# Output transposes behind a run of matmuls, first loads in order of arrival, and a hand-set GpSimd order, in a fused attention and gated-MLP kernel

## The chip, the cores and the metric

The kernel runs on one core of a Trainium2 chip. The metric is the device time of one launch in microseconds (us). The record marks a run as slow when it lies over 1.5% above the fastest of its kernel. Medians and ranges below take in all runs. The profiled span is 2 to 6 us shorter than the timed runs, because it goes from the first instruction to the last.

## The reference, cut to what matters

Attention is within chunks of 64 tokens, then a gated MLP whose gate mixes tokens through a 576 x 576 spatial matrix. Shapes: batch 8, 8 heads, sequence 576, head dimension 64, d_model 512, d_ff 1024, all float32.

```python
scores = scale * (q_c @ k_c.T); attn = softmax(scores); x = attn @ v_c     # per 64-token chunk
h = maximum(x @ w_in, 0)
u, v = h[..., :512], h[..., 512:]
v_n = (v - mean(v)) / sqrt(var(v) + 1e-6)
v_s = einsum('ts,bsd->btd', w_spatial, v_n) + b_spatial[None, :, None]
out = (u * v_s) @ w_out
```

## The kernel before

Work goes by 36 tiles of 128 tokens. For a tile, GpSimd casts q, k and v to bf16. TensorE transposes q and k (TR) and computes scores (QK) and outputs (AV), one step later. Two steps later it transposes the attention output (XT). Then the MLP's matmuls go into a queue (`fifo`) and are emitted by `fill` between the attention parts. They are HV for the half that is normalised, U for the other half, SP for the spatial mix and FIN for the last product. Normalisations (vn) are done on GpSimd in groups of five or four tiles (LN). Ten groups of five "ws" transposes bring the spatial matrix into two layouts. (The texts call the MLP's matmuls MoE matmuls.) TensorE's order is set by the program. The other engines' orders come from a scheduler.

```python
ps_tr = pool("ps_tr", 1, space=PSUM)       # ONE buffer: TR, XT and the ws transposes share it
ps_big = pool("ps_big", 3, space=PSUM)     # HV, U, SP, FIN
# ...
def ws_transpose(p, i):
    ps = ps_tr.tile([128, 1024], BF16, name="tr")
    # five transposes of ws_nat into ps, then
    nc.vector.tensor_copy(dst[:n, :], ps[:n, 0:S])
# ...
load(0); load_w_in(); load(1); load(2); load_ws(); load(3); load_w_out()    # load() also emits the casts
with tc.manual_schedule(engines={mybir.EngineType.PE}):
    # ten ws_transpose pushed, ready at 16 us of a planned clock
    for s in range(NT + 3):
        # ... load(s + 3)
        TR(s)
        XT(s - 2); after_xt(s - 2)         # pushes HV, and U for every fourth tile
        fill(1.5)
        QK(s)
        AV(s - 1)
        fill(1.5)
```

The softmax here doesn't subtract the row's maximum and nothing guards it: scores larger than these inputs give would overflow.

Of the kernel before, what the change touches and what calls it, by code (L numbers as in the profile page):

```python
# [9 lines left out]
BF16 = mybir.dt.bfloat16  # L10
# [6 lines left out]
def kernel(  # L17
# [11 lines left out]
    nc = tc.nc  # L29

    B, H, S, D = q.shape
# [3 lines left out]
    F = d_ff // 2  # L35
    NTOK = B * S
    NT = NTOK // 128
# [9 lines left out]
    persist = pool("persist", 1)  # L47
# [18 lines left out]
    identb = consts.tile([128, 128], BF16, name="identb")  # L66
# [4 lines left out]
    NVB = 6  # L71
    vaug = [persist.tile([128, H, 65], BF16, name=f"vaug{i}") for i in range(NVB)]
# [6 lines left out]

    w_in_sb = persist.tile([128, 4, d_ff], BF16, name="w_in_sb")  # L80
    w_out_sb = persist.tile([128, 4, d_model], BF16, name="w_out_sb")
    ws_nat = [persist.tile([128, S], BF16, name=f"ws_nat{i}") for i in range(5)]

    ws_full = [[persist.tile([128, S], BF16, name=f"wsf{p}_{i}") for i in range(4)]
               for p in (0, 1)]
    ws_tail = [persist.tile([128, S], BF16, name=f"wst{p}") for p in (0, 1)]

    def load_w_in():
        for cb in range(4):
            nc.gpsimd.dma_start(out=w_in_sb[:, cb, :], in_=moe_w_in[cb * 128:(cb + 1) * 128, :])  # L90

    def load_ws():
        for i in range(5):
            n = 128 if i < 4 else 64
            nc.gpsimd.dma_start(out=ws_nat[i][:n, :], in_=moe_w_spatial[i * 128:i * 128 + n, :])
        for p in (0, 1):
            nc.gpsimd.dma_start(out=ws_tail[p][64:65, :], in_=moe_b_spatial[None, :])

    def load_w_out():
        for jb in range(4):  # L100
            nc.gpsimd.dma_start(out=w_out_sb[:, jb, :], in_=moe_w_out[jb * 128:(jb + 1) * 128, :])

    def ws_transpose(p, i):

        if i < 4:
            s0, n, dst = i * 128 + 64 * p, 128, ws_full[p][i]
        else:
            s0, n, dst = (512 if p == 0 else 0), 64, ws_tail[p]
        ps = ps_tr.tile([128, 1024], BF16, name="tr")
        for tb in range(5):  # L110
            m = 128 if tb < 4 else 64
            nc.tensor.transpose(ps[:n, tb * 128:tb * 128 + m],  # L112
                                ws_nat[tb][:m, s0:s0 + n], identb[:m, :m])
        nc.vector.tensor_copy(dst[:n, :], ps[:n, 0:S])


    st = {}
# [8 lines left out]
    def load(t):  # L126
        f32 = {}
        for name, src in (("q", q), ("k", k), ("v", v)):
            f = att_in.tile([128, H, D], FP32, name=f"{name}f")
            for r0, n, b, s in pieces(t):  # L130
                nc.sync.dma_start(out=f[r0:r0 + n], in_=src[b, :, s:s + n, :].rearrange("h s d -> s h d"))  # L131
            f32[name] = f
        qb = att_bf.tile([128, H, D], BF16, name="qb")
        kb = att_bf.tile([128, H, D], BF16, name="kb")
        nc.gpsimd.tensor_copy(qb, f32["q"])  # L135
        nc.gpsimd.tensor_copy(kb, f32["k"])  # L136
        nc.gpsimd.tensor_copy(vaug[t % NVB][:, :, 0:64], f32["v"])  # L137
        st[t] = {"q": qb, "k": kb}

    def TR(t):  # L140
# [40 lines left out]
    def XT(t):  # L181
        x = st[t].pop("x")
        ps = ps_tr.tile([128, 1024], BF16, name="tr")
        for m in range(4):
            nc.tensor.transpose(ps[:, m * 128:(m + 1) * 128],  # L185
                                x[:, 2 * m:2 * m + 2, :].rearrange("p h d -> p (h d)"), identb)
        g, r = divmod(t, 4)
        nc.scalar.copy(xT[g][:, :, r * 128:(r + 1) * 128],  # L188
                       ps[:, 0:512].rearrange("p (m s) -> p m s", m=4))
# [25 lines left out]
    def ln_group(t):  # L215

        k0, j = divmod(t, 9)
        return (2 * k0, j, 5) if j < 5 else (2 * k0 + 1, j - 5, 4)

    def LN(grp):  # L220
        k0 = 9 * (grp // 2)
        n = 5 if grp % 2 == 0 else 4
        ts = [k0 + j + (0 if n == 5 else 5) for j in range(n)]
        m = mv.pop(grp)
        lnv = stat_pool.tile([128, n], FP32, name=f"lnv{n}")
        rstd = stat_pool.tile([128, n], FP32, name=f"rstd{n}")
        nmu = stat_pool.tile([128, n], FP32, name=f"nmu{n}")
        nc.scalar.activation(lnv, m[:, :, 1], AF.Ln, bias=eps_sb)
        nc.scalar.activation(rstd, lnv, AF.Exp, scale=-0.5)
        nc.vector.scalar_tensor_tensor(out=nmu, in0=m[:, :, 0], scalar=-1.0, in1=rstd,  # L230
                                       op0=ALU.mult, op1=ALU.mult)
        for j, t in enumerate(ts):
            vr = relu.pop(t)
            if t - k0 == 4:
                te = tail_pool.tile([128, F], BF16, name="tail_e")
                to = tail_pool.tile([128, F], BF16, name="tail_o")
                nc.gpsimd.memset(te[64:65, :], 1.0)
                nc.gpsimd.memset(to[64:65, :], 1.0)
                nc.gpsimd.tensor_scalar(te[0:64], vr[0:64], rstd[0:64, j:j + 1], nmu[0:64, j:j + 1],
                                        op0=ALU.mult, op1=ALU.add)  # L240
                nc.vector.tensor_scalar(to[0:64], vr[64:128], rstd[64:128, j:j + 1], nmu[64:128, j:j + 1],
                                        op0=ALU.mult, op1=ALU.add)
                tail[grp], tail[grp + 1] = te, to
            else:
                y = vn_pool.tile([128, F], BF16, name="vn")
                nc.gpsimd.tensor_scalar(y, vr, rstd[:, j:j + 1], nmu[:, j:j + 1],  # L246
                                        op0=ALU.mult, op1=ALU.add)
                vn[t] = y
# [50 lines left out]
    def push(ready, cost, emit, after=None):  # L299
        fifo.append([ready, seq[0], cost, emit, after])  # L300
        seq[0] += 1
# [8 lines left out]
    def fill(quota):  # L310
        got = 0.0
        while got < quota:
            ok = [x for x in fifo if x[0] <= clock[0]]
            if not ok:
                break
            it = min(ok, key=lambda x: x[1])
            run(it)
            got += it[2]
# [3 lines left out]
    def after_hv(t):  # L322
        hv_done.add(t)
        grp = ln_group(t)[0]
        n = 5 if grp % 2 == 0 else 4
        k0 = 9 * (grp // 2) + (0 if n == 5 else 5)
        if all(x in hv_done for x in range(k0, k0 + n)):
            LN(grp)
            ln_done.add(grp)
            try_sp()  # L330

    sp_pushed = set()

    def try_sp():
        for b in range(B):
            if b in sp_pushed or b not in ln_done or (b % 2 and b - 1 not in ln_done):
                continue
            last_g = (b * S + S - 1) // 512
            if any((g, fb) not in u_done for g in range(last_g + 1) for fb in range(4)):
                continue  # L340
            sp_pushed.add(b)
            ready = clock[0] + 5.0
            for half in (0, 1):
                for db in range(4):
                    push(ready, 0.62, lambda b=b, half=half, db=db: SP(b, half, db),
                         lambda b=b, half=half, db=db: after_sp(b, half, db))
# [20 lines left out]
    def after_xt(t):  # L367
        push(clock[0] + 1.0, 0.87, lambda t=t: HV(t), lambda t=t: after_hv(t))
        if t % 4 == 3:
            g = t // 4  # L370
            for fb in range(4):
                push(clock[0] + 1.0, 0.87, lambda g=g, fb=fb: U(g, fb),
                     lambda g=g, fb=fb: after_u(g, fb))

    PRE = 4
    load(0)
    load_w_in()
    load(1)
    load(2)
    load_ws()  # L380
    load(3)
    load_w_out()
    with tc.manual_schedule(engines={mybir.EngineType.PE}):
        for p in (0, 1):
            for i in range(5):
                push(16.0, 0.4, lambda p=p, i=i: ws_transpose(p, i))
        for s in range(NT + 3):
            if s + PRE < NT and s > 0:
                load(s + PRE - 1)
            if s == NT - PRE:  # L390
                load(NT - 1)
            if s < NT:
                clock[0] = max(clock[0], 4.0 + 3.6 * s)
                TR(s)
                clock[0] += T_TR
            if 0 <= s - 2 < NT:
                XT(s - 2)
                clock[0] += T_XT
                after_xt(s - 2)
            fill(1.5)  # L400
            if s < NT:
                QK(s)
                clock[0] += T_QK
            if 0 <= s - 1 < NT:
                AV(s - 1)
                clock[0] += T_AV
            fill(1.5)
        while fifo:
            ok = [x for x in fifo if x[0] <= clock[0]]
            run(min(ok, key=lambda x: x[1]) if ok else min(fifo, key=lambda x: (x[0], x[1])))  # L410


# [1 line left out]
_INS = ['q', 'k', 'v', 'moe_w_in', 'moe_w_spatial', 'moe_b_spatial', 'moe_w_out']  # L414
# [26 lines left out]
```

## Time and profile before

| | before |
|---|---|
| time, median (range) | 264.78 us (262.84 to 265.74) |
| profiled span | 259.8 us |
| busy: PE / DVE / ACT / POOL | 200.8 / 119.6 / 107.8 / 103.6 us |
| mean granted clock (see below) | 0.954 |
| qkT copy of tile 6 / 15 / 35 | 48.7 / 97.5 / 216.2 us |

PE is TensorE, DVE VectorE, ACT ScalarE and POOL GpSimd. The granted clock is the share of its full clock that TensorE got. VectorE copies the transposed q and k of each tile once, so the start of that copy says when a tile passed. The page's slices show the stages: 40 equal parts of the span, busy share in tenths, then the granted clock in tenths and the DMA share.

```profile
PE   0425657784887887888888888878888888999993
PEclk9999955997697999999999999999999999999999
DMA  7999999997793812995388968992996030041225
```

The reader should see TensorE half idle in the first eight slices while DMA is full, a clock that falls to 0.5 to 0.7 several times before 85 us, and then a steady 8 in TensorE's row that becomes 9 only near the end.

### The profile page before, as it was taken

To read this page: it belongs to the slowest core of one execution; us is meant where nothing else is said; L and a number is where in the kernel's file an instruction comes from. 1 tells how busy PE (TensorE), PEld (TensorE's weight loads), DVE (VectorE), ACT (ScalarE), POOL (GpSimd) and SP (SyncE) were. 2 spreads that over 40 slices of the span, in tenths; PEclk is the share of its full clock that TensorE was granted. 3 is DMA by queue.
4 is the path that set the end of the run, shared out by engine and by line. 5 is a ranking of instruction groups with operands and counts; after the bars stand their busy time and mean duration, and the time that the engine had idled before them with its cause. 6 is when DMAs were issued, how large, how long until landed. Compare 5 with 4: busy or idle time off the path is not lost.

```text
span 259.8 us, 5942 instructions
## 1 busy us (share of the span) xinstructions
PE 200.8 (77%) x2375; PEld 122.9 (47%) x2402; DVE 119.6 (46%) x305; ACT 107.8 (42%) x197; POOL 103.6 (40%) x173
## 2 busy tenths in 40 slices
PE   0425657784887887888888888878888888999993
PEld 0213444444354654564456445644564456446461
DVE  0222524637434743574257525663374447426160
ACT  1102101563454145526553564256624651661713
POOL 3757553308708093097007631275266000410400
PEclk9999955997697999999999999999999999999999
DMA  7999999997793812995388968992996030041225
GB/s 158 220 231 227 183 213 209 215 201 149 160 219 75 165 42 75 253 207 116 113 201 203 218 160 208 209 158 76 259 232 127 19 145 3 0 159 46 77 85 202
DMA packets 119594, 40.36 MB, mean 155 GB/s; under 512 B 113360, under 2 KB 114448, under 8 KB 119568
## 3 DMA queue, kind: packets, MB, share of 16 engines
q1 hardware_dynamic: 117696, 37.76, 66.7%
q0 software_dynamic: 1872, 2.24, 5.0%
q8 instruction: 18, 0.29, 0.5%
q14 instruction: 8, 0.07, 0.1%
HBM read 32.79 MB, written 9.44 MB: 163 GB/s over the span
## 4 chain that ended last, share of the span: by engine, by line
PE 56%; DVE 19%; POOL 6%; DMA 5%; SPq 5%; ACT 4%; issue 3%; ACTq 0%; POOLq 0%
PE big L285 12%; PE big L253 10%; PE big L269 10%; PE big L203 9%; DVE qkT L148 7%; SPq L131 5%; PE tr L185 5%; DVE bst L209 4%; PE tr L145 3%; DMA kf<-in_k_dram 3%; DVE gat L276 3%; ACT v_relu L206 3%; PE tr L112 2%; PE o L172 2%; PE sc L158 2%
## 5 line engine op out<-in xcount | busy, mean ns | idle before, releaser
L246 POOL TENSOR_SCALAR vn<-v_relu,rstd,nmu 128x512 bf16<-128x512 f32 x32 | 25.3, 799 | 78.5 <-DVE nmu L230 72.5
L188 ACT COPY xT<-tr 128x512 bf16<-128x512 bf16 x36 | 21.1, 586 | 66.5 <-PE tr L185 66.5
L209 DVE BATCH_NORM_STATS2 bst<-v_relu 128x6 f32<-128x512 f32 x36 | 24.9, 692 | 42.5 <-ACT v_relu L206 42.5
L269 PE MATMUL big<-wsf,vn 128*128 128x288 bf16 x256 | 40.3, 286 | 0.1
L203 PE MATMUL big<-w_in_sb,xT 128*128 128x512 bf16 x130 | 38.8, 417 | 1.3 <-issue 0.8
L148 DVE COPY qkT<-tr 128x1024 bf16<-128x1024 bf16 x36 | 24.7, 685 | 32.5 <-PE tr L145 32.5
L185 PE MATMUL tr<-identb,x 128*128 128x128 bf16 x144 | 14.8, 229 | 31.4 <-DVE qkT L148 31.4
L276 DVE TENSOR_TENSOR gat<-big,uT 128x288 bf16<-128x288 f32 (+8 forms) x96 | 30.2, 351 | 15.4 <-PE big L269 14.3
L253 PE MATMUL big<-xT,w_in_sb 128*128 128x512 bf16 x137 | 34.4, 380 | 0.4
L285 PE MATMUL big<-w_out_sb,gat 128*128 128x512 bf16 (+1 forms) x154 | 34.1, 381 | 0.4
L135 POOL CAST qb<-qf 128x512 bf16<-128x512 f32 x36 | 22.1, 614 | 30.3 <-DMA qf<-in_q_dram 24.1
L162 ACT ACTIVATE eT<-sc 128x512 bf16<-128x512 f32 x36 | 21.4, 595 | 26.9 <-PE sc L158 26.9
L206 ACT ACTIVATE v_relu<-big 128x512 f32<-128x512 f32 x36 | 21.5, 597 | 26.4 <-PE big L203 23.8
L185 PEld LDWEIGHTS <-x 128*128 128x128 bf16 x144 | 11.6, 102 | 36.1 <-issue 34.1
L269 PEld LDWEIGHTS <-vn 128*128 128x128 bf16 x256 | 23.9, 97 | 7.8 <-DVE gat L276 0.4
L288 ACT COPY o_sb<-big 128x512 f32<-128x512 f32 x36 | 21.1, 586 | 15.6 <-PE big L285 15.2
L136 POOL CAST kb<-kf 128x512 bf16<-128x512 f32 x36 | 22.1, 614 | 13.4 <-DMA kf<-in_k_dram 13.2
L137 POOL CAST vaug<-vf 128x512 bf16<-128x512 f32 x36 | 22.2, 616 | 8.3 <-DMA vf<-in_v_dram 8.1
L178 DVE TENSOR_TENSOR x<-o,rz 128x512 bf16<-128x512 f32 x36 | 24.9, 691 | 0.9
L255 ACT ACTIVATE uT<-big 128x512 bf16<-128x512 f32 x36 | 21.4, 596 | 9.3 <-PE big L253 9.3
L145 PE MATMUL tr<-identb,qb 128*128 128x128 bf16 x144 | 15.2, 233 | 8.3 <-POOL qb L135 7.2
L203 PEld LDWEIGHTS <-xT 128*128 128x128 bf16 x144 | 14.0, 105 | 14.7 <-issue 3.9
(39 smaller groups left out, 193.5 us busy)
## 6 DMA issues: line engine op xcount, KB each, us to landing
out_dram<-o_sb SPq DMA_DIRECT2D x36, 256.0 KB, 2.1
qf<-in_q_dram SPq DMA_DIRECT2D x32, 256.0 KB, 4.8
kf<-in_k_dram SPq DMA_DIRECT2D x32, 256.0 KB, 5.1
vf<-in_v_dram SPq DMA_DIRECT2D x32, 256.0 KB, 5.2
w_in_sb<-in_moe_w_in_dram POOLq DMA_DIRECT2D x4, 256.0 KB, 5.4
qf<-in_q_dram SPq DMA_DIRECT2D x8, 128.0 KB, 4.7
kf<-in_k_dram SPq DMA_DIRECT2D x8, 128.0 KB, 4.8
vf<-in_v_dram SPq DMA_DIRECT2D x8, 128.0 KB, 4.5
```

Source lines behind the costliest of these rows:

```text
L145: nc.tensor.transpose(ps[:, c:c + 128], st[t][name][:, 2 * m:2 * m + 2, :].rearrange("p h d -> p (h d)"), identb)
L148: nc.vector.tensor_copy(qkT, ps)
L178: nc.vector.tensor_tensor(x, o[:, :, 0:64], rz.to_broadcast([128, H, D]), op=ALU.mult)
L185: nc.tensor.transpose(ps[:, m * 128:(m + 1) * 128], x[:, 2 * m:2 * m + 2, :].rearrange("p h d -> p (h d)"), identb)
L203: nc.tensor.matmul(hv, xT[g][:, cb, r * 128:(r + 1) * 128], w_in_sb[:, cb, F:], start=(cb == 0), stop=(cb == 3))
L206: nc.scalar.activation(vr, hv, AF.Relu)
L209: nc.vector.bn_stats(bst, vr)
L246: nc.gpsimd.tensor_scalar(y, vr, rstd[:, j:j + 1], nmu[:, j:j + 1], op0=ALU.mult, op1=ALU.add)
L253: nc.tensor.matmul(hu, w_in_sb[:, cb, fb * 128:(fb + 1) * 128], xT[g][:, cb, :], start=(cb == 0), stop=(cb == 3))
L269: nc.tensor.matmul(vs[:, 0:HS], lhsT, rhs, start=(i == 0), stop=(i == 4))
L276: nc.vector.tensor_tensor(gat[b][:, db, half * HS + done:half * HS + done + n], vs[:, done:done + n], uT[g][:, db, r:r + n], op=ALU.mult)
L285: nc.tensor.matmul(po[r0:r0 + n, :], gat[b][:, jb, s:s + n], w_out_sb[:, jb, :], start=(jb == 0), stop=(jb == 3))
```

## The change

There are three intents. XT goes behind the run of MLP matmuls, so VectorE's copy out of the single buffer lies beside them. The first tiles are loaded ahead of the weights, and the program's planned clock follows expected arrivals. GpSimd's order is set by hand, with a group's normalisations (`LN_apply`) emitted at the start of the next step, ahead of the cast of tile s+1.

```diff
+    def load_w_in(part, c0, c1): ...      # three transfers in place of four
+    def load_ws(): ...                    # one transfer and a tail in place of five
 ...
-            ready = clock[0] + 5.0
+            ready = clock[0] + 6.0
 ...
-    load(0); load_w_in(); load(1); load(2); load_ws(); load(3); load_w_out()   (cut)
-    with tc.manual_schedule(engines={mybir.EngineType.PE}):
+    ARR = [6.7, 11.0, 18.0, 21.5, 25.0, 32.0, 35.5]
+    with tc.manual_schedule(engines={mybir.EngineType.PE, mybir.EngineType.Pool}):
+        for t in range(PRE):
+            load(t)
+        cast(0, (after_cast0,))            # w_in's transfers between these casts
+        cast(1)
-                push(16.0, 0.4, lambda p=p, i=i: ws_transpose(p, i))
+                push(31.0, 0.4, lambda p=p, i=i: ws_transpose(p, i))
 ...
+            while ln_todo:
+                LN_apply(ln_todo.pop(0))
+            if 0 < s and s + 1 < NT:
+                cast(s + 1)                # load_ws after tile 3, load_w_out after tile 5
             TR(s)
-            XT(s - 2)
             fill(1.5)
+            XT(s - 2)
             QK(s)
             AV(s - 1)
+            # an extra fill and an early XT where the next tile is not expected for 2 us
             fill(1.5)
```

More of the change, by code (lines that the diff above doesn't have):

```diff
@@ L81 @@
     w_out_sb = persist.tile([128, 4, d_model], BF16, name="w_out_sb")
-    ws_nat = [persist.tile([128, S], BF16, name=f"ws_nat{i}") for i in range(5)]
+    ws_nat = persist.tile([128, 5, S], BF16, name="ws_nat")
     ws_full = [[persist.tile([128, S], BF16, name=f"wsf{p}_{i}") for i in range(4)]
@@ L86, with load_w_in @@
     ws_tail = [persist.tile([128, S], BF16, name=f"wst{p}") for p in (0, 1)]
-    def load_w_in():
-        for cb in range(4):
-            nc.gpsimd.dma_start(out=w_in_sb[:, cb, :], in_=moe_w_in[cb * 128:(cb + 1) * 128, :])
+    w_in_v = moe_w_in.rearrange("(c p) f -> p c f", p=128)
+    def load_w_in(part, c0, c1):
+        cols = slice(F, 2 * F) if part == "v" else slice(0, F)
+        nc.gpsimd.dma_start(out=w_in_sb[:, c0:c1, cols], in_=w_in_v[:, c0:c1, cols])
     def load_ws():
-        for i in range(5):
-            n = 128 if i < 4 else 64
-            nc.gpsimd.dma_start(out=ws_nat[i][:n, :], in_=moe_w_spatial[i * 128:i * 128 + n, :])
+        nc.gpsimd.dma_start(out=ws_nat[:, 0:4, :],
+                            in_=moe_w_spatial[0:512, :].rearrange("(i p) s -> p i s", p=128))
+        nc.gpsimd.dma_start(out=ws_nat[:64, 4, :], in_=moe_w_spatial[512:S, :])
         for p in (0, 1):
@@ L99, in load_w_out @@
     def load_w_out():
-        for jb in range(4):
-            nc.gpsimd.dma_start(out=w_out_sb[:, jb, :], in_=moe_w_out[jb * 128:(jb + 1) * 128, :])
+        nc.gpsimd.dma_start(out=w_out_sb, in_=moe_w_out.rearrange("(c p) f -> p c f", p=128))
     def ws_transpose(p, i):
@@ L112, in ws_transpose @@
             nc.tensor.transpose(ps[:n, tb * 128:tb * 128 + m],
-                                ws_nat[tb][:m, s0:s0 + n], identb[:m, :m])
+                                ws_nat[:m, tb, s0:s0 + n], identb[:m, :m])
         nc.vector.tensor_copy(dst[:n, :], ps[:n, 0:S])
@@ L132, in load, with cast @@
             f32[name] = f
+        st[t] = {"f32": f32}
+    def cast(t, after_each=()):
+        f32 = st[t].pop("f32")
         qb = att_bf.tile([128, H, D], BF16, name="qb")
         kb = att_bf.tile([128, H, D], BF16, name="kb")
-        nc.gpsimd.tensor_copy(qb, f32["q"])
-        nc.gpsimd.tensor_copy(kb, f32["k"])
-        nc.gpsimd.tensor_copy(vaug[t % NVB][:, :, 0:64], f32["v"])
+        for dst, name in ((qb, "q"), (kb, "k"), (vaug[t % NVB][:, :, 0:64], "v")):
+            nc.gpsimd.tensor_copy(dst, f32[name])
+            for f in after_each:
+                f(name)
         st[t] = {"q": qb, "k": kb}
@@ L218, in ln_group @@
         return (2 * k0, j, 5) if j < 5 else (2 * k0 + 1, j - 5, 4)
+    ln_st = {}
     def LN(grp):
@@ L231, in LN, with LN_apply @@
                                        op0=ALU.mult, op1=ALU.mult)
+        ln_st[grp] = (k0, ts, rstd, nmu)
+    def LN_apply(grp):
+        k0, ts, rstd, nmu = ln_st.pop(grp)
         for j, t in enumerate(ts):
@@ L328, in after_hv @@
             LN(grp)
+            ln_todo.append(grp)
             ln_done.add(grp)
@@ L332 @@
     sp_pushed = set()
+    ln_todo = []
     def try_sp():
@@ L375, with arrival, after_cast0 @@
     PRE = 4
-    load(0)
-    load_w_in()
-    load(1)
-    load(2)
-    load_ws()
-    load(3)
-    load_w_out()
-    with tc.manual_schedule(engines={mybir.EngineType.PE}):
+    ARR = [6.7, 11.0, 18.0, 21.5, 25.0, 32.0, 35.5]
+    def arrival(t):
+        return ARR[t] if t < len(ARR) else ARR[-1] + 3.5 * (t - len(ARR) + 1)
+    def after_cast0(name):
+        if name == "q":
+            load_w_in("v", 0, 2)
+        elif name == "k":
+            load_w_in("v", 2, 4)
+        else:
+            load_w_in("u", 0, 4)
+    with tc.manual_schedule(engines={mybir.EngineType.PE, mybir.EngineType.Pool}):
[3 more added lines that the diff above has]
+        cast(1)
         for p in (0, 1):
             for i in range(5):
-                push(16.0, 0.4, lambda p=p, i=i: ws_transpose(p, i))
+                push(31.0, 0.4, lambda p=p, i=i: ws_transpose(p, i))
+        xt_next = 0
         for s in range(NT + 3):
-            if s + PRE < NT and s > 0:
+            if PRE <= s + PRE - 1 < NT and s > 0:
                 load(s + PRE - 1)
-            if s == NT - PRE:
-                load(NT - 1)
+            while ln_todo:
+                LN_apply(ln_todo.pop(0))
+            if 0 < s and s + 1 < NT:
+                cast(s + 1)
+                if s + 1 == 3:
+                    load_ws()
+                if s + 1 == 5:
+                    load_w_out()
             if s < NT:
-                clock[0] = max(clock[0], 4.0 + 3.6 * s)
+                a = arrival(s)
+                if a > clock[0]:
+                    fill(a - clock[0] - 0.3)
+                clock[0] = max(clock[0], a)
                 TR(s)
                 clock[0] += T_TR
-            if 0 <= s - 2 < NT:
-                XT(s - 2)
+            fill(1.5)
+            while xt_next <= s - 2 and xt_next < NT:
+                XT(xt_next)
                 clock[0] += T_XT
-                after_xt(s - 2)
-            fill(1.5)
+                after_xt(xt_next)
+                xt_next += 1
             if s < NT:
@@ L406 @@
                 clock[0] += T_AV
+                if s + 1 < NT and arrival(s + 1) > clock[0] + 2.0:
+                    fill(1.5)
+                    clock[0] += 0.5
+                    XT(s - 1)
+                    clock[0] += T_XT
+                    after_xt(s - 1)
+                    xt_next = s
             fill(1.5)
@@ L410 @@
             run(min(ok, key=lambda x: x[1]) if ok else min(fifo, key=lambda x: (x[0], x[1])))
+            while ln_todo:
+                LN_apply(ln_todo.pop(0))
 _INS = ['q', 'k', 'v', 'moe_w_in', 'moe_w_spatial', 'moe_b_spatial', 'moe_w_out']
```

## The prediction

> **What bounds the kernel now.** I read the page's busy shares and slices first, then the windows by stage, then the waits of TensorE, then one step of the timeline. The windows (columns: span of the stretch, busy us of PE, PEld, DVE, ACT, POOL with counts, granted clock, DMA share, GB/s):
>
> ```profile
> 0.00:50.00 50.00, 24.53 (x314) 16.66 (x317) 16.32 (x40) 8.98 (x15) 27.44 (x53) 0.86 1.10 206
> 50.00:100.00 50.00, 39.65 (x517) 24.13 (x521) 24.87 (x60) 23.19 (x44) 23.78 (x39) 0.90 0.73 140
> 100.00:150.00 50.00, 42.80 (x562) 26.47 (x568) 26.92 (x69) 24.62 (x46) 21.93 (x35) 1.00 0.84 183
> 150.00:225.00 75.00, 63.31 (x808) 39.09 (x815) 39.69 (x102) 36.07 (x67) 23.99 (x39) 1.00 0.60 136
> 225.00:260.00 35.00, 30.50 (x182) 16.57 (x183) 11.82 (x35) 14.98 (x27) 6.51 (x9) 1.00 0.28 105
> ```
>
> There are three stages. To 50 us the DMA engines are full (share 1.10) and TensorE is half idle: 50 - 24.5 = 25.5 us. From 50 to 225 us no engine but TensorE is near full; it idles 175 - 145.8 = 29.2 us. After 225 us it is dense, and its 4.5 us of idle is the last copy and store. Busy time here is the union of overlapping records, so I use it for gaps, not for peak. What fills the gaps, from the table of waits over the whole span (us in total, times, longest):
>
> ```profile
> POOL vn L246 <- DVE nmu L230: 72.5, 7, 23.5
> PE tr L185 <- DVE qkT L148: 31.4, 34, 2.4
> PE tr L145 <- POOL qb L135: 7.2, 3, 4.7
> PE tr L145 <- POOL kb L136: 6.8, 3, 3.9
> ```
>
> Restricted to 50 to 225 us, the second row is 27.4 us over 29 waits, so 27.4 of the 29.2 us idle in the long middle stage is one single wait. The timeline shows what it is:
>
> ```profile
> 120.80 0.39 PE L145 MATMUL tr<-identb,kb 128*128 128x128 bf16 x4
> 121.22 0.69 DVE L148 COPY qkT<-tr 128x1024 bf16<-128x1024 bf16 x1 [0.56 <-PE tr L145]
> 121.97 0.38 PE L185 MATMUL tr<-identb,x 128*128 128x128 bf16 x4 [0.78 <-DVE qkT L148]
> 122.19 1.89 PE L253 MATMUL big<-xT,w_in_sb 128*128 128x512 bf16 x7
> ```
>
> The pool of transposes holds one PSUM buffer. TensorE transposes q and k of tile s into it (TR), and the next thing in its program is the transpose of output tile s-2 (XT) into the same buffer. So it stands still for VectorE's copy (0.69 us plus hand-over), with eight MoE matmuls ready behind it. A step, from one qkT copy to the next, is 5.67 us where nothing else disturbs it (121.22 back from 115.55).
>
> **What the Trainium skill says.** "PSUM — Partial Sum Buffer", section "Engine vs sequencer instructions": matmuls start and complete in program order, and the queues of ScalarE, VectorE and GpSimd are strict FIFO. The trace agrees: XT holds back the ready L253 matmuls. "Perfetto Trace Analysis", section "Matmuls" under "Optimizing Tensor Performance": independent groups should rotate through PSUM banks so that evacuation of one overlaps matmuls of the next. The one "tr" buffer doesn't, at 0.78 us a time. "TensorE: Matmul & The Clock Gate", Part 1: the clock is halved until the array has been busy for about 3.4 us. The first group of four q transposes takes 0.60 us, against 0.39 us in the step above, so the DMA-fed beginning does run cold. "DMA: Bandwidth & Descriptors", section "Why small descriptors are slow (HBM only)": there is a fixed cost per packet and per descriptor at 256 B. The page counts 113360 of 119594 packets under 512 B, and the saturated rate is 206 GB/s.
>
> **Part 1, XT behind the fill.** The order becomes TR(s), a run of about 1.7 us of MoE matmuls, XT(s-2), QK(s), AV(s-1), another run. The copy (0.78 us of wait, up to 1.3 us where VectorE is late) then lies beside 1.7 us of matmuls. Nothing is added. QK reads qkT, long done, and XT's buffer is copied out by ScalarE (0.59 us) under QK, AV and the next run, 0.75 + 1.7 us, before the next TR. The undisturbed step becomes 5.67 - 0.78 = 4.89 us. I count 90% of the 27.4 us as recovered, **-24.5 us**: some steps have an empty queue of MoE work early (the short steps near 48, 62 and 78 us), and in steps of spatial matmuls VectorE runs at about 90%. There six evictions of about 0.48 us plus qkT 0.69, x 0.69 and reciprocal 0.20 make 4.5 us in 4.89.
>
> **Part 2, the beginning.** Weights now follow the casts: w_in in three transfers after the three casts of tile 0, the spatial weights after tile 3's casts, w_out after tile 5's. About 1.33 + 1.05 MB of reads, at 206 GB/s some 11.6 us of DMA, move behind the first tiles. Before, qkT copies of tiles 4 and 5 stand at 35.1 and 46.2 us. A tile is 786 KB, 3.8 us at 206 GB/s, and the change expects tiles 4 and 5 at 25 and 32 us. The ten spatial-weight transposes (1.3 us each through the single buffer, 26 to 42 us before) remain, and they remain slow. By 50 us the kernel before has copied tile 6; I expect tile 8 or 9 after. Two to three tiles of work at about 3 us (attention 1.25, first matmul's two halves 0.87 + 0.87, by the chain's durations) are done earlier: **-8 us** of idle, including an extra XT placed where the next tile has not come.
>
> **Part 3, GpSimd by hand.** Before, casts may run ahead of a group's normalisations. In the new program order the normalisations of a group (LN_apply) stand ahead of the cast of the next tile but one. GpSimd cannot pass them. The chain of waits shows how late their input is:
>
> ```profile
> 186.89 0.88 PE big L203 x4
> 187.85 0.61 ACT v_relu L206
> 188.48 0.69 DVE bst L209
> 189.62 0.30 ACT lnv L228
> 190.53 0.16 DVE nmu L230
> ```
>
> From the end of the last group member's matmuls (187.77) to nmu's end (190.69) is 2.9 us. Then GpSimd works 4 x 0.80 = 3.2 us, or with tail and memsets 3.2 + 0.76 + 2 x 0.52 = 5.0 us, then two casts of 0.61 us. So the casts are done h + 7.5 or h + 9.3 us into a pair of steps, where h is when those matmuls ended, and TR wants them at 2 x 4.89 = 9.8 us. With h between 1.3 and 4.9 the stall is 0 to 2.6 us for groups of four tiles and 0.8 to 4.4 us for groups of five. Averaging about 1.1 and 2.7 over six groups that still have tiles behind them gives 11 us. Where h falls early it vanishes, and the wait for a clogged GpSimd (first row of the second table) that starved loads between 78 and 102 us goes, so I charge **+6 us** net.
>
> **Part 4, DMA in the middle.** In a 4.89 us step it must bring 786 KB (3.8 us) and store 256 KB (an estimate of 0.7 us, from 105 GB/s at share 0.28 in the last row of windows). That is 4.5 us, 92%. I charge **+3 us** for late tiles and VectorE-limited steps together.
>
> **Sum.** 259.8 - 24.5 - 8 + 6 + 3 = 236.3 us of span. The timed runs (262.84 to 265.74) stand 3 to 6 us above the profiled span, and the profiled run itself 2.1; I add 3. **Predicted: 239 us.**
>
> **Rivals.** (a) The wait only moves: GpSimd becomes the bound at each group. For it: the order is now forced and the working gives up to 4.4 us a group. Against: GpSimd is only 40% busy and has three cast buffers. If all 11 to 20 us fell on the path, 246 to 253 us. (b) DMA becomes the bound. For it: 92% in the middle and a full first stage. Inputs alone need 28.3 MB / 206 GB/s = 137 us, the weights about 13 (cast transfers' share), some 22 stores 15, so the last tile cannot come before about 166 us, and TensorE wants it near 172. Against: buffers reach up to seven tiles ahead. This would give 242 to 248 us. (c) All parts work and the early work makes the clock warm sooner (0.86 and 0.90 in the first two rows), while stalls vanish: 227 us. (d) XT's delay puts off HV and the MoE queue runs dry, so the gap is only moved: it would stay near 255 us. The queue is rarely dry after 80 us (all 5.67 us steps hold full runs), so this is unlikely.
>
> **Range and chances.** (c) and (a) set the edges: 227 to 251 us. The removed wait alone is 10% of the span, so faster by over 2% (under 259.8 us) gets 0.95, same 0.04, slower 0.01.
>
> **What would show it.** Right: the row "tr L185 <- qkT" falls from 31.4 us to under 5; undisturbed steps are near 4.9 us; TensorE idle in the first 50 us falls to 15-20 us; new rows of "tr L145 <- qb" or "kb" of 1 to 4 us appear after each group's normalisations. Wrong: steps stay over 5.4 us, or waits for qb and kb in the middle add up to more than 12 us, or they trace back to transfers in flight rather than to L246.

## The result, and the profile after

The changed kernel takes 249.01 us in the median (248.57 to 251.08) against 264.78 us. The ratio is 0.9429, 95% interval 0.9353 to 0.9504. Here and below a ratio is the mean time of one kernel's fast runs over that of the other's in the same rounds, so it is not quite the ratio of the medians quoted. The time is inside the predicted range (227 to 251 us), but near its slow end. The sum foretold 23.5 us off the span, and 12.5 us came (259.8 to 247.3).

The windows of the changed kernel (columns as in the prediction):

```profile
0.00:50.00 50.00, 24.93 (x310) 16.35 (x310) 15.58 (x39) 8.59 (x14) 22.13 (x41) 0.89 1.09 194
50.00:100.00 50.00, 40.80 (x551) 25.25 (x551) 25.47 (x62) 21.65 (x42) 25.11 (x42) 0.84 0.86 169
100.00:150.00 50.00, 48.05 (x604) 29.32 (x603) 28.75 (x73) 27.37 (x52) 22.41 (x36) 1.00 0.77 175
150.00:225.00 75.00, 72.40 (x822) 42.76 (x821) 42.51 (x109) 42.03 (x80) 28.62 (x45) 1.00 0.62 149
225.00:260.00 35.00, 18.15 (x122) 11.09 (x120) 7.84 (x24) 5.91 (x11) 2.44 (x4) 0.96 0.18 68
```

TensorE's busy time rose by 5.3 us in the 50 us from 100 and by 9.1 us in the 75 us from 150, but only by 0.4 and 1.2 us in the two windows before. (The 0.89 in the first row counts the time before the clock's first record, at 31.8 us, as 1.00.) Progress by tiles says it more sharply. The qkT copy of tile 15 starts at 97.51 us before and at 97.50 us after. **By then nothing had been gained.** From tile 15 to tile 35 the kernel before takes 118.7 us, 5.94 a tile. The changed one takes 104.5 us, 5.23 a tile. That is 14.2 us, more than the whole gain: what comes after the start of tile 35's copy takes 45.3 us, against 43.6 before.

The waits of the changed kernel (us in total, times, longest), to set against the four in the prediction:

```profile
POOL vn L258 <- DVE nmu L238: 64.3, 6, 16.2
PE tr L151 <- POOL qb L141: 17.2, 9, 5.1
PE tr L151 <- POOL kb L141: 5.8, 9, 2.9
PE tr L191 <- DVE qkT L154: 2.3, 3, 1.0
```

XT's wait fell from 31.4 to 2.3 us, but the waits for casts of q and k rose from 14.0 to 23.0 us. In both kernels 14.0 us of these fall in the first 50 us; the new 9.0 us come later. One step of the timeline shows the first (instructions of TensorE and VectorE alone; a bracket gives the engine's idle time and who ended it):

```profile
122.24 0.39 PE L151 MATMUL tr<-identb,kb 128*128 128x128 bf16 x4
122.46 1.03 PE L265 MATMUL big<-xT,w_in_sb 128*128 128x512 bf16 x4
122.66 0.69 DVE L154 COPY qkT<-tr 128x1024 bf16<-128x1024 bf16 x1 [1.34 <-PE tr L151]
123.42 1.05 PE L297 MATMUL big<-w_out_sb,gat 128*64 128x512 bf16 x8
124.40 0.40 PE L191 MATMUL tr<-identb,x 128*128 128x128 bf16 x4
```

While VectorE copies, TensorE does MLP matmuls, and XT no longer carries an idle time in brackets. An undisturbed step (tile 15 to 16) is 4.73 us, against 5.67 before.

The second, at tile 9, from the timeline (lines left out between). It shows one of the places where the first half's gain went:

```profile
62.65 3.22 POOL L258 TENSOR_SCALAR vn<-v_relu,rstd,nmu 128x512 bf16<-128x512 f32 x4 [12.35 <-DVE nmu L238]
62.86 0.42 PE L178 MATMUL o<-vaug,eT 64*64 64x65 bf16 x16
67.71 0.60 POOL L141 CAST qb<-qf 128x512 bf16<-128x512 f32 x1
68.37 0.61 PE L151 MATMUL tr<-identb,qb 128*128 128x128 bf16 x4 [5.09 <-POOL qb L141]
69.33 1.91 PE L209 MATMUL big<-w_in_sb,xT 128*128 128x512 bf16 x4
73.02 1.03 PE L209 MATMUL big<-w_in_sb,xT 128*128 128x512 bf16 x4
```

GpSimd was idle for 12.35 us, waiting for the group's nmu, with the cast of tile 9 behind that wait in its order. Then it spent 5.1 us on the group. TensorE had an empty queue of MLP work and stood still for 5.09 us. The clock fell in this stall, at 65.9 us, and was 0.50 from 66 to 72 us: four HV matmuls took 1.91 us, and 1.03 once the clock was back. At tile 13 the same thing cost 2.19 us.

### The profile page after: what moved, and what is told of

Its sections match the earlier page's. It is cut to its first block, busy times and chain, and to the rows that moved or that the text cites. A ratio compares the mean times of both kernels' runs of the same rounds, so it can differ in the third digit from the quotient of the medians.

```text
span 247.3 us, 5971 instructions
## 1 busy us (share of the span) xinstructions
PE 204.3 (83%) x2402; PEld 124.8 (50%) x2402; DVE 120.2 (49%) x305; ACT 105.6 (43%) x197; POOL 100.7 (41%) x166
## 3 DMA queue, kind: packets, MB, share of 16 engines
q1 hardware_dynamic: 117696, 37.76, 69.7%
## 4 chain that ended last, share of the span: by engine, by line
PE 49%; POOL 7%; issue 5%; DMA 4%; DVE 3%; SPq 2%; ACT 1%; POOLq 0%; ACTq 0%
PE big L281 13%; PE big L297 10%; PE big L265 9%; PE big L209 8%; DMA vf<-in_v_dram 4%; PE tr L151 4%; PE o L178 2%; PE tr L191 2%; PE sc L164 2%; SPq L132 2%; POOL vn L258 2%; POOL kb L141 2%; POOL qb L141 2%; DVE bst L215 1%; POOL vaug L141 1%
## 5 line engine op out<-in xcount | busy, mean ns | idle before, releaser
L258 POOL TENSOR_SCALAR vn<-v_relu,rstd,nmu 128x512 bf16<-128x512 f32 x32 | 25.1, 796 | 81.4 <-DVE nmu L238 64.3
L209 PE MATMUL big<-w_in_sb,xT 128*128 128x512 bf16 x144 | 40.6, 414 | 0.0
L265 PE MATMUL big<-xT,w_in_sb 128*128 128x512 bf16 x144 | 35.6, 390 | 0.0
L297 PE MATMUL big<-w_out_sb,gat 128*128 128x512 bf16 (+1 forms) x160 | 34.5, 381 | 0.0
L168 ACT ACTIVATE eT<-sc 128x512 bf16<-128x512 f32 x36 | 22.0, 611 | 17.5 <-PE sc L164 17.5
L281 PEld LDWEIGHTS <-vn 128*128 128x128 bf16 x256 | 23.7, 97 | 10.6 <-DVE gat L288 2.5
L151 PEld LDWEIGHTS <-qb 128*128 128x128 bf16 x144 | 11.1, 105 | 25.2 <-POOL qb L141 19.2
L265 PEld LDWEIGHTS <-w_in_sb 128*128 128x128 bf16 x144 | 13.5, 100 | 14.7 <-issue 1.6
```

The costliest lines, as they stand in the source:

```text
L151: nc.tensor.transpose(ps[:, c:c + 128], st[t][name][:, 2 * m:2 * m + 2, :].rearrange("p h d -> p (h d)"), identb)
L168: nc.scalar.activation(eT, sc[:, :, 0:256], AF.Exp, scale=att_scale)
L209: nc.tensor.matmul(hv, xT[g][:, cb, r * 128:(r + 1) * 128], w_in_sb[:, cb, F:], start=(cb == 0), stop=(cb == 3))
L258: nc.gpsimd.tensor_scalar(y, vr, rstd[:, j:j + 1], nmu[:, j:j + 1], op0=ALU.mult, op1=ALU.add)
L265: nc.tensor.matmul(hu, w_in_sb[:, cb, fb * 128:(fb + 1) * 128], xT[g][:, cb, :], start=(cb == 0), stop=(cb == 3))
L281: nc.tensor.matmul(vs[:, 0:HS], lhsT, rhs, start=(i == 0), stop=(i == 4))
```

## The experiments

Twelve kernels ran, each on one chip. All gave correct results. Lines are compared within a call where possible, and across calls by their ratios to the kernel before. Timings are medians of four runs. The diffs are shortened.

### Which part carries the gain

**e1_xt_only**, the kernel before with one edit:

```diff
-            if 0 <= s - 2 < NT:
-                XT(s - 2); clock[0] += T_XT; after_xt(s - 2)
             fill(1.5)
+            if 0 <= s - 2 < NT:
+                XT(s - 2); clock[0] += T_XT; after_xt(s - 2)
             if s < NT:
                 QK(s)
```

> The kernel before with one edit: XT(s-2) stands behind the first run of MoE matmuls. Theory A (the move of XT carries the whole gain; the load order and the GpSimd order add nothing): the row of waits 'tr <- qkT' of XT falls from 31.4 us to under 4, and the time is 245 to 251 us, like the changed kernel's 249. Theory B (each of the three parts carries some): 254 to 259 us.

Measured: 243.31 us (242.62 to 244.52), ratio 0.9263 (0.9177 to 0.9348). This is below theory A's range: the one edit is faster than the whole change. Its waits of TensorE:

```profile
PE tr L145 <- POOL qb L135: 13.7, 7, 4.8
PE tr L145 <- POOL kb L136: 9.1, 6, 3.2
PE tr L185 <- DVE qkT L148: 2.3, 4, 0.8
```

XT's wait is gone here too (31.4 to 2.3). But 22.8 us now go to q and k casts, against 14.0 before. A faster TensorE reaches the casts sooner and waits there (15.7 us before 50 us, 7.1 us after). So 29.1 us of wait removed, less 8.8 us of new waiting, is 20.3 us, and the span fell by 18.1 (259.8 to 241.7).

**e2_xt_first**, the changed kernel with XT put back:

```diff
-            fill(1.5)
             while xt_next <= s - 2 and xt_next < NT:
                 XT(xt_next); ...
+            fill(1.5)
```

> The changed kernel with XT put back ahead of the run. Theory A: the XT wait is back at 27 to 32 us and the time is 262 to 268 us, no better than the kernel before. Theory B: 254 to 259 us, since the other two parts still give their share.

Measured: 283.64 us (282.52 to 283.88), ratio 1.0789 (1.071 to 1.0868). Both theories missed the time; the XT wait, 27.5 us, is in theory A's range. **Without the XT move the other two parts make the kernel 8% slower than it was.** Its waits:

```profile
PE tr L191 <- DVE qkT L154: 27.5, 32, 1.4
PE tr L151 <- POOL qb L141: 24.6, 8, 5.1
PE tr L151 <- POOL kb L141: 4.2, 5, 2.6
```

The casts cost 28.8 us here, 14.8 more than before, and the clock in the window from 50 to 100 us is 0.74 against 0.90. TensorE's busy time is 209.1 us against 200.8 for the same matmuls. The parts don't add. By the ratios the XT move is worth 1 - 0.9263 = 0.074 of some 262 us, or 19 us, in the old order, and 1.0789 - 0.9429 = 0.136, or 36 us, in the new one.

### GpSimd's order

**e3_pool_free** leaves GpSimd to the scheduler again:

```diff
-    with tc.manual_schedule(engines={mybir.EngineType.PE, mybir.EngineType.Pool}):
+    with tc.manual_schedule(engines={mybir.EngineType.PE}):
```

> The changed kernel with GpSimd's order left to the scheduler; the orders of all other engines are the same but for a few VectorE rows. Theory A (the hand order costs: TR of tile 9 waited 5.1 us and of tile 13 2.2 us for casts that stood behind a group's normalisations): those two waits shrink and the time is 242 to 247 us. Theory B (the hand order helps by letting normalisations come in time): 251 to 256 us, with new waits for qb or kb, or for vn.

Measured: 246.24 us (245.51 to 247.3), ratio 0.9377 (0.9304 to 0.945). It is inside theory A's range, but its interval overlaps the changed kernel's, so taken alone it decides nothing. Of theory A's two waits one is gone; that of tile 13 stayed at 2.19 us. The beginning was slower (tile 6 is copied at 52.3 us, against 47.4), so the time mixes a loss and a gain.

**e4_cast_first** changes two blocks' order in the hand order:

```diff
-            while ln_todo:
-                LN_apply(ln_todo.pop(0))
             if 0 < s and s + 1 < NT:
                 cast(s + 1)
                 ...
+            while ln_todo:
+                LN_apply(ln_todo.pop(0))
```

> The changed kernel with the cast of tile s+1 ahead of the waiting normalisations in GpSimd's hand order; only GpSimd's order changes. Theory A: the waits for qb at tiles 9 and 13 (5.1 and 2.2 us) and the idle DMA between 60 and 68 us go, with the cold clock that follows them: 241 to 246 us. Theory B: the normalisations come one cast (1.9 us) later and the MoE queue runs dry instead: 248 to 251 us.

Measured: 240.78 us (239.68 to 241.76), ratio 0.9165 (0.9092 to 0.9238). Theory A's range was met. TensorE's, ScalarE's and the DMA queue's orders are the same as in the changed kernel. The change's order, normalisations ahead of the cast, therefore cost 0.9429 / 0.9165, that is 2.9%. The waits for qb from 50 to 100 us, in the changed kernel and then in e4:

```profile
PE tr L151 <- POOL qb L141: 7.3, 2, 5.1
PE tr L151 <- POOL qb L141: 2.1, 1, 2.1
```

A hand order is not bad in itself: with the cast first it beats the scheduler's (e3) by 5.5 us on the same chip.

### The new beginning

**e5_old_start** gives the changed kernel the old beginning, the weights' old pieces among it, and keeps the hand order:

```diff
-        for t in range(PRE): load(t)
-        cast(0, (after_cast0,)); cast(1)
+        load(0); cast(0); load_w_in(); load(1); cast(1); load(2); load_ws(); load(3); cast(2); load_w_out()
-                push(31.0, 0.4, ...ws_transpose...)
+                push(16.0, 0.4, ...ws_transpose...)
-                a = arrival(s); fill(...); clock[0] = max(clock[0], a)
+                clock[0] = max(clock[0], 4.0 + 3.6 * s)
-                (the extra fill and early XT)
```

> The changed kernel with the beginning of the kernel before: weight transfers in their old pieces and places, spatial-weight transposes from 16 us on, the old pacing rule, no extra XT; GpSimd's hand order with normalisations ahead of casts stays. Theory A (the new beginning gives next to nothing, the forced order costs): 246 to 251 us, within 2% of the changed kernel's 249, with waits for qb and kb after 50 us of 5 us or more. Theory B (the new beginning saved the forecast 8 us and the forced order ate it): 254 to 259 us.

Measured: 247.93 us (247.47 to 248.23), ratio 0.9433 (0.9375 to 0.9491), against the changed kernel's 0.9429. Theory A: no difference, and 8.2 us of waits for qb and kb from 50 to 225 us.

**e6_old_start_cast_first** is e5 with the cast-first edit of e4.

> As e5_old_start, and the cast ahead of the normalisations as in e4_cast_first. It differs from e4_cast_first (240.8 us) by the beginning alone. Theory A: 240 to 244 us, as the XT move alone in the old order (243.3) with the free order replaced by a harmless one. Theory B (new beginning worth 8 us): 247 to 250 us.

Measured: 237.83 us (237.13 to 238.81), ratio 0.9041 (0.8973 to 0.911). It is below theory A's range, and 10.1 us faster than e5 on the same chip. So the order of normalisations and casts costs 4% under the old beginning too. Against e4 (0.9165), which differs by the beginning alone, the old beginning is, if anything, the better one. The intervals just overlap.

### The ten transposes of the spatial matrix

The forecast of 8 us for the beginning had failed, and the timeline of the changed kernel showed a chain there:

```profile
36.29 0.52 PE L113 MATMUL tr<-identb,ws_nat 128*128 128x128 bf16 x5 [1.12 <-DVE qkT L154]
36.84 0.46 DVE L115 COPY wsf<-tr 128x576 bf16<-128x576 bf16 x1 [0.61 <-PE tr L113]
37.35 0.52 PE L113 MATMUL tr<-identb,ws_nat 128*128 128x128 bf16 x5 [0.55 <-DVE wsf L115]
37.91 0.46 DVE L115 COPY wsf<-tr 128x576 bf16<-128x576 bf16 x1 [0.61 <-PE tr L113]
```

It goes on so to 50.2 us, broken only by one tile's transposes and scores: half a microsecond of TensorE, half a microsecond of waiting for the copy. The granted clock over 36 to 51 us was 0.59. Tile 6's casts were done at 38.3 us, and its TR started at 46.4.

**e7_ws_big** is e4 with one word changed for the ten:

```diff
     def ws_transpose(p, i):
-        ps = ps_tr.tile([128, 1024], BF16, name="tr")
+        ps = ps_big.tile([128, 1024], BF16, name="big")
```

> e4_cast_first with the ten spatial-weight transposes in the pool of three PSUM buffers instead of the single one shared with TR and XT. Theory A (the forecast saving at the beginning was lost to this serial chain, ten times 1.3 us from 36 to 50 us, in which tile 6's TR stood 8 us behind its casts): the ten take under 8 us, the qkT copy of tile 6 comes at 42 to 44 us instead of 47, and the time falls by 2 to 5 us to 236 to 239 us. Theory B (the beginning is bound by arrivals, so nothing is gained): 240 to 242 us.

Measured: 232.05 us (230.17 to 234.12), ratio 0.8807 (0.8721 to 0.8893). Theory A's direction, and more than its size: 3.9% against e4's 0.9165. In its timeline:

```profile
34.55 2.05 PE L113 MATMUL big<-identb,ws_nat 128*128 128x128 bf16 x20
35.58 1.54 DVE L115 COPY wsf<-big 128x576 bf16<-128x576 bf16 x4
```

Twenty transposes now take 2.05 us. All ten groups are through at 40.4 us, tile 6's copy comes at 39.6 us (47.0 in e4), tile 8's at 50.3 (61.2 in e4). From 31.3 us, where both have a record, to 50 us the clock is 1.00 (0.68 in e4). Shorter waits and a warm clock come together, and no run separates them.

**e8_ws_spread** also spreads the ten over about 35 us of the planned clock:

```diff
-                push(31.0, 0.4, lambda p=p, i=i: ws_transpose(p, i))
+                push(31.0 + 3.5 * (5 * p + i), 0.4, lambda p=p, i=i: ws_transpose(p, i))
```

> e7_ws_big with the ten spatial-weight transposes spread, one about every 3.5 us of the planned clock, instead of in a row. They are first needed near 75 to 90 us. Theory A: TR of tiles 6 and 7 no longer stands behind them, their copies come at 38 to 45 us, and the time is 234 to 238 us. Theory B (arrivals bind): as e4_cast_first, 240 to 242 us, TensorE simply waiting for casts instead.

Measured: 234.43 us (232.67 to 237.06), ratio 0.8855 (0.8773 to 0.8936). It is in theory A's range against e4, but it gains nothing over e7. With the three buffers, then, that the ten stand in a row costs nothing that these runs can tell. Spreading them in the single buffer was not run.

**e12_before_ws_big** makes e7's edit alone in the kernel before.

> The kernel before with the spatial-weight transposes alone moved to the pool of three buffers; XT stays ahead of the run. Theory A: the chain costs the same with or without the XT move, 251 to 257 us against 262 to 265. Theory B: 260 to 265 us, its waits lie beside the wait for arrivals.

Measured: 258.08 us (255.95 to 263.09), ratio 0.9799 (0.9713 to 0.9884). It lies between the two theories: 5.8 us by the medians, where theory A asked for 7 or more. The interval leaves a gain of 1.2 to 2.9%, and the verdict at 2% is unclear. Tile 6 is copied at 42.7 us against 48.7, but at tile 15 the lead is 4.2 us (93.3 against 97.5).

### Putting together

**e9_cast_two** is e7 with the casts one step further ahead (`cast(s + 2)` in step s, `cast(2)` in the prologue, the weight loads still after tiles 3 and 5):

```diff
-            if 0 < s and s + 1 < NT:
-                cast(s + 1)
+            if 0 < s and s + 2 < NT:
+                cast(s + 2)
```

> e7_ws_big (232.1 us) with the casts of a tile one more step ahead in GpSimd's order (cast s+2 in step s, ahead of the waiting normalisations). Theory A (in e7 tile 10's TR still waits 3.8 us for a cast that stands behind the first group's normalisations, so a cast further ahead takes that wait away): no wait for qb or kb over 1.5 us after 50 us, 227 to 230 us. Theory B (that wait was for the transfer, or the normalisations now come too late): 231 to 234 us.

Measured: 229.87 us (227.69 to 231.71), ratio 0.8724 (0.8644 to 0.8804). It has the lowest ratio of all, 7.5% under the changed kernel (0.8724 / 0.9429), but its interval overlaps those of e7, e8 and e10, so the step from e7 is not settled by the time. One wait over the bound set by theory A stayed: 2.30 us at tile 11, in place of 3.81 us at tile 10. The casts of the tile behind the normalisations still wait for the group's 4.9 us on GpSimd (56.2 to 61.1 us). Going a step further ahead moved the wait by a tile and made it shorter. The clock row is flat, where the kernel before dips several times. It is flat by record from 30.5 us on; before, four q transposes take 0.61 us, against 0.40 later. This profile is of the fastest of the four runs (227.69 us, mean clock 0.998; the others have 0.961 to 0.983):

```profile
PEclk9999999999999999999999999999999999999999
```

**e10_old_start_ws_big** is e7 with the old beginning (e6 with the ws edit).

> e7_ws_big with the beginning of the kernel before (weight transfers, pacing, no extra XT). Theory A (the new beginning is worth nothing in itself; e6 was no slower than e4): 229 to 233 us, within 2% of e7's 232. Theory B (the new beginning pays once the serial chain of spatial-weight transposes is out of the way, as forecast): 237 to 241 us.

Measured: 230.93 us (229.54 to 235.5), ratio 0.8775 (0.8689 to 0.886), against e7's 0.8807. Theory A. The new load order does bring tile 4 forward (28.3 us in e7 against 33.1), but at tile 9 the two stand at 53.3 and 53.6, and at tile 12 both at 69.7. In both the DMA engines are full for the first 50 us (share 1.09). That the weights put off must still come in that time is the likely reason; no run tests it.

**e11_before_xt_ws_big** is the kernel before with e1's and e7's edits and nothing else.

> The kernel before with two edits only: XT behind the run of matmuls, and the ten spatial-weight transposes in the pool of three buffers; GpSimd's order left to the scheduler. Theory A (the two serial uses of the single PSUM buffer are what cost): 231 to 236 us, 8 us or so under e1's 243. Theory B (the chain mattered only under the new beginning, which puts it later): 240 to 244 us.

Measured: 234.98 us (234.23 to 236.78), ratio 0.8937 (0.887 to 0.9004), in theory A's range. Two edits of a few lines take off 10.6%, where the whole change took 5.7%.

## Why the prediction was right or wrong, point by point

- **The bound and part 1 (XT) were right in mechanism.** The row fell from 31.4 to 2.3 us, where under 5 was forecast, and an undisturbed step went to 4.73 us, where 4.89 was forecast. The size was too high: "90% of the 27.4 us as recovered" took no account of the waits for casts that an earlier TensorE runs into. By itself (e1) the part took 18.1 us off the span, against 24.5.
- **Part 2 failed.** Its step "By 50 us the kernel before has copied tile 6; I expect tile 8 or 9 after" did not hold. At 50 us both kernels had copied tile 6 and not tile 7, and idle time in the first 50 us was 25.1 us, not 15 to 20. The error was to note that the ten ws transposes "remain, and they remain slow" and to charge nothing for it. The early tiles did come sooner: tile 5 is copied at 35.6 us, against 46.2. But the ten, moved behind tile 5, then held tile 6 back by 8 us, at a granted clock of 0.59, and the lead was down to 1.3 us. With that chain gone (e7) tile 8 is copied at 50.3 us. The load order itself was worth nothing in three pairs (e5 against the changed kernel, e6 against e4, e10 against e7). In the last pair the chain is gone, so to charge for it would not have saved the 8 us: the step that a few early tiles shorten the whole failed too.
- **Part 3 was right in mechanism, with the size at the low end and the place wrong.** The forced order costs 2.9% (changed kernel against e4) to 4% (e5 against e6), some 7 to 10 us, where +6 was charged. The averaging "over six groups" was wrong: only the first two groups stalled TensorE for over half a microsecond, by 5.09 and 2.19 us, and from 100 us on the waits for qb and kb add up to 1.6 us. What the working left out is the MLP queue. At tile 9 it is empty, so TensorE comes for the next tile early. Later it fills the steps, and the casts come at most 0.44 us late. The working also left out the clock, which fell in the first stall (65.9 us) and after the second (86.4 us).
- **Part 4 held.** No wait of TensorE led back to a transfer after 100 us. DMA shares there are 0.77 and 0.62, not 0.92. VectorE cost 2.6 us, in two waits for gat in SP steps. Rival (b), DMA as the bound, falls for the middle of the run. Rival (d), a queue run dry by XT's delay, falls too: e2, with XT first, stalls at tile 9 for the same 5.09 us.
- **Rival (a)**, "246 to 253 us" if the GpSimd stall fell on the path, hit the total by luck: the forced order cost 7 to 10 us and not its "11 to 20 us", and parts 1 and 2 gave less than forecast. Rival (c), 227 us, is approached only with both faults mended (e9, 229.87 us). The 0.86 that it quotes as the clock of the first 50 us counts the time without a record as warm.
- **The range and the chances held** (249.01 in 227 to 251; faster). The predicted time was 10 us too fast. Parts 1, 2 and 3 taken singly miss by 6, 8 and 1 to 4 us, which is more than that: the parts don't add, as e2 shows, and a sum of single terms could not have been exact.

What stays open: how the loss in the stalls divides into waiting and cold clock, and why e2's casts cost so much more than the changed kernel's. The profile shows that four of e2's groups stall TensorE after 50 us (5.09, 4.82, 2.86 and 2.71 us), each time with the casts behind the normalisations on GpSimd. Why the later groups stall too was not tested.

## What to carry to other kernels

When one PSUM buffer serves several uses, list them all: each copy out of it held TensorE here unless other matmuls stood between (0.78 us for XT, 0.55 us for a ws group), and the second use (ten transposes at the start) was worth nearly half as much as the first (0.033 of the time from e1 to e11, 0.074 for e1). When an engine's order is set by hand, put what others wait for ahead of what itself waits. A stall at a time when the queue of other work is empty can be paid twice, since the clock may fall in it or after it, as it did with both such stalls of the changed kernel. And a mean of the clock is worth no more than its record: look where that begins.

## What the Trainium skill lacked or had wrong

- "TensorE: Matmul & The Clock Gate", Part 4 (PE-mode transpose), says that the full clock does not engage for transposes. In e7 the ten groups from 34.5 to 40.4 us, 5.02 us of transposes in 5.84 us, ran at a granted clock of 1.00 (window 34 to 41 us, TensorE busy 6.59 of 7.00), 217 ns a transpose. In the changed kernel, with pauses of 0.55 us between groups, the clock over 36 to 51 us was 0.59 and a transpose took 268 ns. That the pauses made the difference is likely, but was not tested apart from the buffers.
- The same page, section "Why this matters for your kernels", gives about 3 us as the idle gap that costs the clock. In the changed kernel a gap of 2.19 us was enough (clock 0.61 in the two microseconds from 86 us, four HV matmuls 1.91 us); in the 3.42 us up to the fall TensorE was busy for 1.07. In e9 a gap of 2.30 us was not (clock 1.00). The gap's length alone does not tell.
- No page says that a profile's clock record can begin tens of microseconds into the run (28.1 us in the kernel before, 49.6 in e1), so that a mean over it reads 1.00 where the matmuls' durations show half speed (0.74 to 0.80 us for five transposes in e1, 0.52 at a recorded 1.00 in the changed kernel).
